# Loads into alternating partitions, pads ahead of the last stage, and a new order, in a linear attention with a mixture of experts

## Chip, cores and metric
One core of a Trainium2 chip. The metric is the device time of one launch in microseconds, the median of several runs.

## What is computed
```python
q_s = softmax(q, axis=-1)                 # q, k, v: 8 batches x 8 heads x 576 rows x 64, fp32
k_s = softmax(k, axis=2)                  # over the 576 rows
attn = einsum('bhsd,bhde->bhse', q_s, einsum('bhsd,bhse->bhde', k_s, v))
x = attn.transpose(0, 2, 1, 3).reshape(4608, 512)
idx = argmax(x @ w_gate, axis=1)          # 8 experts; gate = the largest softmax probability
y[t] = relu(x[t] @ w1[idx[t]]) @ w2[idx[t]]      # w1: 8 x 512 x 1024, w2: 8 x 1024 x 512
out = gate[:, None] * y
```

## The kernel before
The program has two stages. The first computes the attention of the eight batches, routes every row to its expert and scatters it, 512 values with its gate and row number (520 columns), into a DRAM buffer `xs` that has a region per expert. The second, `experts`, walks over tiles of up to 384 rows of `xs`, multiplies them with their expert's weights (each fp32 product as three products of a high and a low part) and scatters the result to `out`. In between, SP fills the 128 rows behind each expert's last row with zeros, the pads (L1232 to L1235), and waits for them before it loads the first tile (`xload`, L1181).

A batch has 576 = 4.5 x 128 rows. Before the change `rows` (L138) cuts them in two contiguous blocks: one half of the partitions (0 to 63, or 64 to 127) holds five rows each, the other half four. k and v have the fives in the lower half; q has them in the lower half in even batches and in the upper half in odd ones, so that the leftover rows of two batches fill one tile of 128. Each tensor of a batch takes two DMAs, one for each half (`lk`, `lv`, `lq`); the first batch's k takes four. All are issued by SP, whose queue also carries parts of the first expert's w1 (L654) and w2 (L665). k has four buffers, v has two (VS) and q has one (QT), so a q load waits for the exponentials of the batch before.

Per batch: VectorE takes the maximum of k over the rows in pieces (`f0`: L292, L293; `f1`: L296, the fifth row of the lower half), PE transposes it, VectorE reduces it (L305), PE spreads it over the partitions (L310), VectorE subtracts it (L326) and ScalarE takes the exponential (L330): five instructions each, four for a pair of heads (KS, KE: 512 columns) and one for the fifth rows (KR, ER: 64 partitions, 512 columns). ScalarE copies v to VT beside columns of ones (`vp` L162, `vq` L165). PE multiplies k and v (L355), five slots x 8 heads; the ones give the sums. For q VectorE takes the maximum of a row (L425, one instruction per batch), GpSimd subtracts it (L430) and ScalarE takes the exponentials, of one slot already on the untransposed rows (L444). A tile of 128 rows is transposed on PE (TR, L470), copied by ScalarE (EX, L475), multiplied with kv and the gate weights (MM, L482), divided on VectorE (DE, RE, EV: L490 to L501) and routed by some fifteen small VectorE steps (R0 to RH); POOL scatters it (PU, L610). After the last batch VectorE computes the tables that the second stage walks by (T1 to T8). T1 also writes `padi`, the row at which each expert's pad begins (L754). The first 384 rows of expert 0 already go through their first layer here (L1 to L3: L711 to L718).

The order of all this is a list written out by hand, `ORDER` (L29): each word names a step, and `Plan.emit` issues the steps in that order, so the list sets the order on every engine and in SP's queue. At the border to the second stage all engines meet. PE then multiplies two dummy tiles (`first(0)`, `first(1)`, L995), transposes the first tile (`tr`, L935), and runs a third dummy before the loop over the experts (L949, L965).

Of the kernel before, what the change touches and what calls it, by code (L numbers as in the profile page):

```python
# [16 lines left out]
P = 128  # L17
# [16 lines left out]
LV KM0 VP MM LV KS MM N0 DE N1 VQ RE KM1 N2 LV EV KM2 TR KM3 DE QM TR EX G0 EX KM4 G1 ER G2 RE QS KS EV KV G3 KE KR KE MM KS QS
QE LS QE KV DE KM0 QE KV QE RE KS VQ LQ MM R0 VP LQ KS CZ KM0 KV LV LK TR EV LK LV TR EX KM1 R8 N0 KM2 DE R1 RE R9 N1 MM KE RC
R3 EV EX N2 KM3 MM DE R4 RE QM TR TR EX R5 G0 EX EV KM4 G1 QS ER QMR MM KE KS DE KV RB QE QS KS QE RE TR R6 EV QSR KE KV KR QE
RH G2 DE QE R7 RE_ RE KS VP LQ KV EV LQ LK KS KV LK RG LS LV KE TR WG RA G3 RD ER R0 MM KM0 VQ EX R8 N0 DE RF R1 PU N1 TR EX KM0
MM N2 PU R3 RE R4 KM1 QM VQ KV RH PU KE G0 KE R5 KV R9 EX EV KE QS KM2 WH RC MM DE RB RE G1 R6 EV G2 RA QE RE_ DE QS KM3 QE TR
RE RD RG PU EV QE MM QE KM0 EX KV LQ G3 LQ DE VP RF RE PU TR KM0 WG KV EV PU MM EX N0 KM1 TR LS PU MM DE N1 EX R0 RE R8 N2 EV TR
R1 R7 MM DE R3 RE R4 EV RH WL EX TR QM WH G0 EX WL WG R9 LK G1 KM2 LK WH KM4 LV QMR QS LV DE KM3 KS KM4 WH KS G2 PU KE RE KR KE  # L40
MM KS G3 QS ER KS QE KV QSR KR QE EV KE KV WL KE KS R5 KV DE KS KE WL QE KS KV QE RB RE PU KM0 TR ER LQ MM VQ LQ EV WG EX LV VP
N0 KS MM LV RC RD WG DE RE_ N1 TR WG RA RG RE RF DE EV PU TR EX N2 KM0 TR MM PU LS RE EX KV R0 PU KM1 EX R8 QM G0 KE PU KM2 KE
KV KE G1 KV R1 EV QS VQ WH TR R3 DE KM3 MM R9 RC RE R6 R4 QE RE_ R7 KM4 RA EV QS QE R5 KV KS EX WL WH MM RB DE KR RG RD RH ER RE
G2 RF KS PU QE EV TR QE G3 KS PU LQ KE MM WG DE KS WH LQ EX RE PU N0 TR EV TR EX N1 MM DE WL N2 RE EV TR LS WL MM DE R0 RE EX EV
WH PU G0 R8 R6 EX DE MM R1 RE R7 R9 R3 VP R4 EV RH PU R5 TR RB RC MM RE_ DE RD RA RG RF RE PU QM G1 KV KE KE G2 PU EX KV G3 EV
# [38 lines left out]
def attention_moe(ctx: ExitStack, tc: tile.TileContext, q, k, v, w_gate, w1, w2, xs, out):  # L84
# [51 lines left out]
    HALF = (slice(0, REM), slice(REM, P))  # L136

    def rows(src, b, i, fives):  # L138
        n = SLOT if i == fives else FULL
        lo = REM * (SLOT if fives == 0 else FULL) if i else 0  # L140
        return n, src[b, :, lo:lo + REM * n, :].rearrange("h (p j) d -> p h j d", j=n)

    def load(b):
# [20 lines left out]
        def vq():  # L164
            ACT(VT[i][:REM, :, FULL // 2 * VW:FULL // 2 * VW + D], o.vs[:REM, :, FULL, :], AF.Copy)  # L165
# [11 lines left out]
        add("VQ", b, 0, ACTE, vq, [("LV", b, 0)] + rng("KV", b - 2, NP))  # L177
# [7 lines left out]
    TS(ident, ji, 0.0, None, op0=ALU.is_equal)  # L185
    ones = cst.tile([E, E], F32, name="ones")
# [40 lines left out]
    def consts():  # L227
        for g in range(B // 2):
            for i in range(2):
                base = (2 * g + i) * S  # L230
                lo = i * (FULL + 1)
                for h in range(2):
                    n = SLOT if h == i else FULL
                    start = base + (REM * (SLOT if i == 0 else FULL) if h else 0)
                    iota(tok[HALF[h], g, lo:lo + FULL], pattern=[[1, FULL]], base=start, channel_multiplier=n)
                    if h == i:
                        iota(tok[HALF[h], g, FULL:FULL + 1], pattern=[[1, 1]], base=start + FULL, channel_multiplier=n)
# [23 lines left out]
    def more_consts():  # L261
        TS(before, ji, 0.0, None, op0=ALU.is_gt)
# [20 lines left out]
    def kmax(b):  # L283
# [11 lines left out]
        def f1():  # L295
            TT(o.km[:REM], o.km[:REM], o.kt[:REM, :, FULL, :], op=ALU.max)  # L296
# [17 lines left out]
        add("KM1", b, 0, DVE, f1, [("LK", b, 0 if b else 2), ("KM0", b, parts - 1)])  # L314
        add("KM2", b, 0, PE, f2, [("KM1", b, 0)], take="tr", until=[("KM3", b, 0)])
        add("KM3", b, 0, DVE, f3, [("KM2", b, 0), ("KM4", b - 2, 0)])
        add("KM4", b, 0, PE, f4, [("KM3", b, 0)], take="tr", until=rng("KS", b, NP - KS_POOL[b]) + [("KR", b, 0)] + ([("KB", b, 0)] if KS_POOL[b] else []))

    def kval(b):
# [3 lines left out]
        def sub(h0, h1, r, j0, j1):  # L323
            t = o.kt[:r, h0:h1, j0:j1, :]
            mb = o.mb.rearrange("p c (i d) -> p (c i) d", i=2)
            TT(t, t, mb[:r, h0:h1, None, :].to_broadcast([r, h1 - h0, j1 - j0, D]), op=ALU.subtract)  # L326

        def ex(h0, h1, r, j0, j1):
            t = o.kt[:r, h0:h1, j0:j1, :]
            ACT(t, t, AF.Exp)  # L330
# [15 lines left out]
        def kv(c):  # L346
# [108 lines left out]
    def xtiles(b):  # L455
# [279 lines left out]
    def tables():  # L735
# [75 lines left out]

        add("T0", z, 0, PE, t0, [("R7", *done[z, SLOT])], take="sm", until=[("T1", z, 0)])
# [61 lines left out]
    with tc.tile_pool(name="qs", bufs=1, space=PSUM) as qs, tc.tile_pool(name="bx", bufs=1) as bx:  # L874
# [8 lines left out]
                            XT=XT, PT=PT, PH=PH, PY=PY, ident=ident, ones16=ones16, tab=tab, zr=zr, padi=padi, w1=w1, w2=w2, xs=xs, out=out, **vars(I0))  # L883
# [5 lines left out]
def experts(nc, tc, g):  # L889
# [10 lines left out]
    sB, sBT, sPad = sem("sb"), sem("sbt"), sem("spad")  # L900
# [273 lines left out]
    def sp():  # L1174
# [57 lines left out]
        for n in range(E):  # L1232
            row = e.value_load(g.padi[0:1, n:n + 1], min_val=0, max_val=E * RS)  # L1233
# [45 lines left out]
```

## Time and profile before
| | us |
|---|---|
| median of 3 runs (lowest, highest) | 669.83 (668.38, 672.86) |
| the profiled execution | 669.31 |
| its span, first to last instruction | 667.4 |
| first stage, to the landing of the last scatter | 226.94 |
| border, to PE's first transpose | 245.26 |
| PE busy in the span | 588.9 |
| mean granted TensorE clock, share of 2.4 GHz | 0.944 |

Times in the profile run from the first instruction. A busy PE is not PE at its peak. A wait for several events is put down to the one that came last.

### The profile page before, as it was taken

To read this page: it belongs to the slowest core of one execution; us is meant where nothing else is said; L and a number is where in the kernel's file an instruction comes from. 1 tells how busy PE (TensorE), PEld (TensorE's weight loads), DVE (VectorE), ACT (ScalarE), POOL (GpSimd) and SP (SyncE) were. 2 spreads that over 40 slices of the span, in tenths; PEclk is the share of its full clock that TensorE was granted. 3 is DMA by queue.
4 is the path that set the end of the run, shared out by engine and by line. 5 is a ranking of instruction groups with operands and counts; after the bars stand their busy time and mean duration, and the time that the engine had idled before them with its cause. 6 is when DMAs were issued, how large, how long until landed. Compare 5 with 4: busy or idle time off the path is not lost.

```text
span 667.4 us, 11339 instructions
## 1 busy us (share of the span) xinstructions
PE 588.9 (88%) x3766; PEld 523.4 (78%) x3767; DVE 330.6 (50%) x704; ACT 257.0 (39%) x519; POOL 134.6 (20%) x218
## 2 busy tenths in 40 slices
PE   3777676878779679999999999999999999999993
PEld 1556565767678469898989898989989898898993
DVE  4665684876858404326442323233751662653472
ACT  0555564565544012224422222214432542442552
POOL 4120133656634301101010101010101101101010
PEclk9687786889999789999999999999999999999998
DMA  9999999997453279210661203020462165044000
GB/s 184 205 198 205 215 220 246 214 232 184 160 184 141 101 200 318 52 45 17 204 185 35 62 17 78 16 63 16 100 235 63 44 184 176 11 154 157 16 19 4
DMA packets 64716, 86.09 MB, mean 129 GB/s; under 512 B 8623, under 2 KB 50095, under 8 KB 64048
## 3 DMA queue, kind: packets, MB, share of 16 engines
q1 hardware_dynamic: 58688, 66.71, 42.8%
q0 software_dynamic: 6000, 19.03, 7.5%
q8 instruction: 15, 0.25, 0.2%
q14 instruction: 13, 0.11, 0.1%
HBM read 63.78 MB, written 22.74 MB: 130 GB/s over the span
## 4 chain that ended last, share of the span: by engine, by line
PE 62%; SPq 1%; DMA 1%; issue 1%; POOL 0%; ACT 0%; POOLq 0%
PE py L965 29%; PE pt L949 16%; PE ph L949 16%; PE py L995 1%; SPq L1233 1%; DMA xt<-xs 0%; SPq L1234 0%; PE pt L935 0%; DMA xs<-xr,posi 0%; DMA xs<-zr 0%; SPq L922 0%; POOL out L1150 0%; SPq L1186 0%; ACT yt L1023 0%; SPq L1256 0%
## 5 line engine op out<-in xcount | busy, mean ns | idle before, releaser
L965 PE MATMUL py<-w2h,hid 128*128 128x512 f32 x576 | 179.7, 389 | 0.0
L965 PEld LDWEIGHTS py<-w2h,hid 128*128 128x128 f32 x576 | 108.1, 188 | 22.1
L1150 POOL DMA_INDIRECT out<-yt,ix x39 | 43.3, 1110 | 352.5 <-ACT yt L1023 352.5
L965 PE MATMUL py<-w2l,hid 128*128 128x512 f32 x288 | 112.1, 389 | 0.0
L1097 DVE SCALAR_TENSOR_TENSOR hid<-pt,hid 128x384 fp32r<-128x384 f32 x56 | 30.9, 558 | 148.9 <-ACT hid L1032 141.0
L1023 ACT ACTIVATE yt<-py,ga 128x512 f32<-128x512 f32 x39 | 26.8, 688 | 150.4 <-PE py L965 133.8
L482 PE MATMUL xp<-kx,qTs 128*128 128x146 f32 x256 | 45.3, 328 | 23.7 <-DVE xr L501 16.5
L965 PEld LDWEIGHTS py<-w2l,hid 128*128 128x128 f32 x288 | 54.1, 188 | 10.7
L1097 DVE SCALAR_TENSOR_TENSOR hid<-ph,hid 128x384 fp32r<-128x384 f32 x56 | 31.2, 558 | 59.1 <-ACT hid L1032 59.1
L482 PEld LDWEIGHTS xp<-kx,qTs 128*128 128x128 f32 x256 | 39.4, 218 | 26.6 <-DVE xr L501 13.2
L1032 ACT ACTIVATE hid<-ph 128x384 fp32r<-128x384 f32 x56 | 27.6, 492 | 65.7 <-PE ph L949 65.7
L1032 ACT ACTIVATE hid<-pt 128x384 fp32r<-128x384 f32 x56 | 27.6, 492 | 65.0 <-PE pt L949 62.6
L610 POOL DMA_INDIRECT xs<-xr,posi x36 | 39.5, 1098 | 50.5 <-DVE posi L599 18.5
L1087 DVE STREAM_TRANSPOSE xx<-xb 128x1536 f32<-128x1536 f32 x14 | 40.7, 2908 | 7.7 <-DVE gs L1093 5.7
L949 PE MATMUL pt<-xl,w1h 128*128 128x384 f32 (+1 forms) x224 | 43.8, 317 | 0.0
L949 PE MATMUL ph<-xh,w1l 128*128 128x384 f32 (+1 forms) x224 | 43.6, 316 | 0.0
L949 PE MATMUL pt<-xh,w1l 128*128 128x384 f32 (+1 forms) x224 | 43.6, 316 | 0.0
L949 PE MATMUL ph<-xh,w1h 128*128 128x384 f32 (+1 forms) x224 | 43.6, 316 | 0.0
L949 PE MATMUL ph<-xl,w1h 128*128 128x384 f32 (+1 forms) x224 | 43.6, 316 | 0.0
L949 PE MATMUL pt<-xh,w1h 128*128 128x384 f32 (+1 forms) x224 | 43.6, 316 | 0.0
L430 POOL TENSOR_TENSOR qs<-qt,qm 128x1024 f32<-128x1024 f32 (+1 forms) x16 | 23.5, 1484 | 77.3 <-DVE qm L425 26.4
L355 PE MATMUL kv<-vt,kt 128*64 128x65 f32 (+1 forms) x640 | 35.3, 257 | 3.4 <-ACT vt L162 3.1
(205 smaller groups left out, 954.5 us busy)
## 6 DMA issues: line engine op xcount, KB each, us to landing
raw<-in_moe_w SPq DMA_DIRECT2D x10, 2048.0 KB, 8.2
xb<-xs SPq DMA_DIRECT2D x32, 192.0 KB
qt<-in_q SPq DMA_DIRECT2D x8, 640.0 KB
vs<-in_v SPq DMA_DIRECT2D x8, 640.0 KB, 14.3
kt<-in_k SPq DMA_DIRECT2D x7, 640.0 KB, 15.1
qt<-in_q SPq DMA_DIRECT2D x8, 512.0 KB
vs<-in_v SPq DMA_DIRECT2D x8, 512.0 KB, 15.9
kt<-in_k SPq DMA_DIRECT2D x7, 512.0 KB, 17.1
```

Source lines behind the costliest of these rows:

```text
L355: nc.tensor.matmul(o.kv[i * D:(i + 1) * D, c, lo:lo + D + 1], o.kt[:r, 2 * c + i, j, :], VT[b % 2][:r, 2 * c + i, at:at + D + 1], start=Fa ...
L430: nc.gpsimd.tensor_tensor(o.qs[:, j0:j1].rearrange("p j h d -> p h j d"), o.qt[:, :, j0:j1, :], o.qm[:, :, j0:j1, None].to_broadcast([P, H ...
L482: nc.tensor.matmul(xv[:, c, :KW], o.qT[i][:, c, :], kx[:, c, :], start=True, stop=True)
L610: s = nc.gpsimd.indirect_dma_start(out=xs, out_offset=bass.IndirectOffsetOnAxis(ap=n.pi[:, t - t0:t - t0 + 1], axis=0), in_=xr[:, t, :], i ...
L949: m = e.matmul(ph, wt[:, c, f * P:(f + 1) * P], xt[:, c, :w], start=(n == 0), stop=(n == 3 * NC - 1))
L965: m = e.matmul(g.PY[u], ht[:, f, u * P:(u + 1) * P], wt[:, f, :], start=(n == 0), stop=(n == 3 * NF - 1))
L995: m = e.matmul(g.PY[u], ht[:, f, u * P:(u + 1) * P], wt[:, f, :], start=(n == 0), stop=(n == 3 * NF - 1))
L1023: m = e.activation(g.YT[u], g.PY[u], AF.Copy, scale=g.GA[:, u:u + 1]).wait_op(sPY[u], cu[u], GE)
L1032: e.activation(g.HH[:, f, :], g.PH[f][:, :W], AF.Relu).wait_op(sPH[f], it, GE).then_inc(sHH[f], 1)
L1087: e.transpose(g.XX, g.XB.rearrange("p t (a c) -> p c t a", c=NC)).wait_op(sB, b80, GE)
L1097: e.scalar_tensor_tensor(g.HL[:, f, :], g.PH[f][:, :W], 0.0, g.HH[:, f, :].bitcast(F32), op0=ALU.max, op1=ALU.subtract).wait_op(sHH[f], it ...
L1150: e.indirect_dma_start(out=g.out, out_offset=bass.IndirectOffsetOnAxis(ap=g.IX[:, u:u + 1], axis=0), in_=g.YT[u], in_offset=None, bounds_c ...
```

## The change
Nine consecutive rows now belong to a pair of partitions. The even partition takes the first five, the odd one the last four; for k both take five, so the fifth is there twice. Each tensor still takes two DMAs, one for the even and one for the odd partitions, each of 64 partitions with a step of two. Doubling k's fifth row does no harm to the maximum; in the product it must count once, so v's first slot is zero on the odd partitions (VS is cleared once) and so is the column of ones beside it, which is set from a new constant `par`, the parity of the partition. With every partition holding five rows of k, the steps KR and ER go, and KS and KE take 640 columns. In odd batches q's fives go to the odd partitions; the transposed copy of the leftover tile then sorts even and odd columns into two halves. The row numbers `tok` follow the new layout.

The pads move from `experts` to a step PD of the first stage, after T1, without a wait of their own. `ORDER` is replaced as a whole; its last lines now hold PD.

```diff
-    def rows(src, b, i, fives):
-        n = SLOT if i == fives else FULL
-        lo = REM * (SLOT if fives == 0 else FULL) if i else 0
-        return n, src[b, :, lo:lo + REM * n, :].rearrange("h (p j) d -> p h j d", j=n)
+    ODDS = (slice(0, P, 2), slice(1, P, 2))
+
+    def rows(src, b, lo, hi, hs=slice(0, H)):
+        return src[b, hs].rearrange("h (m r) d -> m h r d", r=FULL + SLOT)[:, :, lo:hi, :]
...
-            n, src = rows(k, b, p % 2, 0)
-            nc.sync.dma_start(o.kt[HALF[p % 2], hs, :n, :], src[:, hs])
+            lo = p % 2 * FULL
+            nc.sync.dma_start(o.kt[ODDS[p % 2], hs], rows(k, b, lo, lo + SLOT, hs))
...
-            n, src = rows(v, b, p, 0)
-            nc.sync.dma_start(o.vs[HALF[p], :, :n, :], src)
+            nc.sync.dma_start(o.vs[ODDS[p], :, p:, :], rows(v, b, p * SLOT, p * FULL + SLOT))
...
-            n, src = rows(q, b, p, i)
-            nc.sync.dma_start(QT[HALF[p], :, :n, :], src)
+            n = FULL if p else SLOT
+            nc.sync.dma_start(QT[ODDS[p ^ i], :, :n, :], rows(q, b, p * SLOT, p * SLOT + n))
...
+    par = cst.tile([P, 4], F32, name="par")
+    RED(par[:, 0:1], ident[:, 1:P:2], op=ALU.add, axis=AX.X)
+    TS(par[:, 1:2], par[:, 0:1], -1.0, 1.0, op0=ALU.mult, op1=ALU.add)
...
+        nc.vector.memset(VS[i][:, :, 0, :], 0.0)
+        nc.vector.tensor_copy(VT[i][:, :, 0], par[:, 1:2].to_broadcast([P, H]))
...
-            TT(o.km[:REM], o.km[:REM], o.kt[:REM, :, FULL, :], op=ALU.max)
+            TT(o.km, o.km, o.kt[:, :, FULL, :], op=ALU.max)
...
-        add("KR", b, 0, DVE, lambda: sub(0, H, REM, FULL, SLOT), [("KM4", b, 0)])
-        add("ER", b, 0, ACTE, lambda: ex(0, H, REM, FULL, SLOT), [("KR", b, 0)])
...
-                add("KS", b, c, DVE, lambda c=c: sub(2 * c, 2 * c + 2, P, 0, FULL), [("KM4", b, 0)])
+                add("KS", b, c, DVE, lambda c=c: sub(c), [("KM4", b, 0)])
...
-            ACT(o.qT[i], o.qP[i], AF.Copy if FULL - ON_ACT[b] <= slots[i] < FULL else AF.Exp)
+            to = o.qT[i] if slots[i] < FULL else o.qT[i].rearrange("p c (a m) -> p c m a", a=2)
+            at = o.qP[i] if slots[i] < FULL else o.qP[i].rearrange("p c (m a) -> p c m a", a=2)
+            ACT(to, at, AF.Copy if FULL - ON_ACT[b] <= slots[i] < FULL else AF.Exp)
...
+        def pads():
+            for e in range(E):
+                row = nc.sync.value_load(padi[0:1, e:e + 1], min_val=0, max_val=E * RS)
+                d = nc.sync.dma_start(xs[bass.ds(row, P), :], zr)
+                for other in written:
+                    tc.declare_no_dep(d.ins, other.ins, reason="distinct rows")
+                written.append(d)
+
+        add("PD", z, 0, SP, pads, [("T1", z, 0)])
...
-        for n in range(E):
-            row = e.value_load(g.padi[0:1, n:n + 1], min_val=0, max_val=E * RS)
-            e.dma_start(g.xs[bass.ds(row, P), :], g.zr).then_inc(sPad, 16)
-        e.wait_ge(sPad, 16 * E)
         xload(0)
...
-PU RE_ RF RD L3 R7 VL PU T0 L1 L2 RG R9 VH RH RC T1 RH PU L3 RA T2 RF RE_ T3 PU L1 L2 L3 T5 PU L1 L2 PU IM PU L3 L2 T6 T7 L1 L3
+T1 RF R5 T2 PD RB L3 T3 L1 PU RA RE_ RD T5 PU L1 L2 PU VH VH L3 T6 RG VL L2 L1 RF L3 PU T7 VL L1 L2 PU L3 T8 IN VL L2 L3
```

SP at the start of the program, before: the loads of the first batches' q (qt), v (vs0, vs1 of even and odd batches) and k (kt), with partitions, heads and columns of each.
```order
L169 DMA qt_90<-in_q 64x8x320
L169 DMA qt_90<-in_q 64x8x256
L158 DMA vs0_88<-in_v 64x8x320
L158 DMA vs0_88<-in_v 64x8x256
L153 DMA kt_189<-in_k 64x8x320
L153 DMA kt_189<-in_k 64x8x256
L153 DMA kt_198<-in_k 64x8x320
L153 DMA kt_198<-in_k 64x8x256
L158 DMA vs1_89<-in_v 64x8x320
L254 DMA wg_105<-in_moe_w_gate 64x4x8 x2
```
The same place after the change, from the first q on.
```order
L166 DMA qt_95<-in_q 64x8x320
L166 DMA qt_95<-in_q 64x8x256
L151 DMA kt_188<-in_k 64x8x320 x2
L155 DMA vs0_93<-in_v 64x8x320
L155 DMA vs0_93<-in_v 64x8x256
L151 DMA kt_197<-in_k 64x8x320 x2
```
The second k comes before the first v, and both halves of k have 320 columns.

SP at the end of the first stage, before: the last loads of that stage, the meeting of the engines (NO_OP, branch) and the first pad, which reads padi.
```order
L692 DMA xt<-xs 128x520 x3
L665 DMA raw_2077<-in_moe_w 128x2x512 x4
L884 NO_OP
L1256 UNCONDITIONAL_BRANCH
L1233 TENSOR_LOAD padi
L1233 ISA x2
L1234 ISA
L1234 DMA xs<-zr 128x520
```
After the change, from the same loads on to the first pad.
```order
L694 DMA xt<-xs 128x520 x3
L667 DMA raw_2090<-in_moe_w 128x2x512 x4
L816 TENSOR_LOAD padi
L816 ISA x2
L817 ISA
L817 DMA xs<-zr 128x520
```
The eight pads (one is shown) stand ahead of the meeting; behind the meeting SP's next rows are now the table reads and `xload`.

VectorE around the step that writes padi, before.
```order
L602 RECIPROCAL xr_116<-own 128x3
L590 TENSOR_REDUCE own<-pe 128x2
L752 TENSOR_SCALAR c_169<-cn,r_128 128x1
L753 COPY c_169<-cn 128x7
L754 TENSOR_TENSOR padi<-cn,padc 1x8
L718 SCALAR_TENSOR_TENSOR hid<-ph_2263,hid 128x384
L583 TENSOR_SCALAR cm<-own 128x2
L757 TENSOR_SCALAR g<-c_169,thr 128x8
```
The same place after the change.
```order
L592 TENSOR_REDUCE own<-pe 128x2
L578 TENSOR_TENSOR acc_5_2291<-acc_3_2282,own 128x8
L754 TENSOR_SCALAR c_170<-cn,r_137 128x1
L755 COPY c_170<-cn 128x7
L756 TENSOR_TENSOR padi<-cn,padc 1x8
L601 TENSOR_TENSOR posi<-own,cm 128x3
L759 TENSOR_SCALAR g<-c_170,thr 128x8
L589 TENSOR_TENSOR rs<-rk,oh 128x16
```
padi now follows the last count of rows (acc) at once; routing steps that stood ahead of it stand behind it.

## Rows read from the trace of the kernel before
**Rows 1.** The page's slices: the span in 40 equal parts of 16.7 us; busy tenths of PE, VectorE and the DMA engines, and GB/s.
```profile
PE   3777676878779679999999999999999999999993
...
DVE  4665684876858404326442323233751662653472
...
DMA  9999999997453279210661203020462165044000
GB/s 184 205 198 205 215 220 246 214 232 184 160 184 141 101 200 318 52 45 17 204 185 35 62 17 78 16 63 16 100 235 63 44 184 176 11 154 157 16 19 4
```
**Rows 2.** Windows over the first stage: length, busy us (and instructions) of PE, PE's weight loads, DVE, ACT, POOL, then the granted TensorE clock, the DMA share and GB/s.
```profile
0.00:120.00 120.00, 80.55 (x730) 63.38 (x733) 71.48 (x179) 59.16 (x143) 30.73 (x82) 0.82 1.10 211
120.00:227.00 107.00, 83.58 (x748) 73.30 (x742) 78.19 (x293) 55.26 (x136) 57.18 (x84) 0.92 0.63 174
0.00:227.00 227.00, 164.13 (x1472) 136.68 (x1473) 149.67 (x472) 114.42 (x279) 87.91 (x165) 0.87 0.88 194
```
**Rows 3.** The chain that ended last: start, us, what.
```profile
224.22 2.72 DMA xs<-xr,posi
...
228.26 0.47 SPq L1233
...
238.98 0.39 SPq L922
...
242.12 3.10 DMA xt<-xs
245.26 2.83 PE pt L935 x12
...
651.70 5.50 PE py L965 x24
```
**Rows 4.** Windows by the rate of the DMA engines, columns as in rows 2: the first load's first half microsecond, the loads behind it, two stretches of loads alone, loads beside scatters, a load of w2 (128 partitions), a load of raw weights (128 partitions).
```profile
2.90:3.40 0.50, 0.30 (x1) 0.00 (x0) 0.00 (x0) 0.00 (x0) 0.41 (x5) 1.00 1.00 365
3.40:5.00 1.60, 0.00 (x0) 0.00 (x0) 0.00 (x0) 0.00 (x0) 1.23 (x11) 1.00 1.13 232
30.00:40.00 10.00, 7.72 (x43) 5.15 (x42) 6.50 (x11) 5.17 (x15) 0.00 (x0) 0.85 1.15 197
50.00:60.00 10.00, 6.61 (x85) 5.64 (x82) 5.30 (x15) 4.50 (x10) 0.00 (x0) 0.84 1.13 204
...
148.00:150.00 2.00, 2.00 (x12) 1.67 (x14) 2.00 (x4) 1.10 (x2) 0.42 (x1) 0.50 1.03 379
194.00:195.00 1.00, 0.50 (x4) 0.50 (x5) 0.00 (x0) 0.45 (x1) 0.82 (x4) 1.00 1.12 387
251.00:255.00 4.00, 4.00 (x22) 3.57 (x20) 3.23 (x3) 0.69 (x1) 0.99 (x1) 1.00 1.01 426
```
**Rows 5.** VectorE's maximum of q, one per batch: all eight by their line (shortest, median and longest ns, first and last start), then the second, sixth, seventh and eighth as the timeline has them.
```profile
L425 DVE TENSOR_REDUCE qm<-qt x8: 2233/2280/2286, 14.9 to 171.4; 128x32 f32<-128x2048 f32 x8
...
42.40 2.29 DVE L425 TENSOR_REDUCE qm<-qt 128x32 f32<-128x2048 f32 x1 [4.42 <-DMA qt<-in_q]
...
125.80 2.27 DVE L425 TENSOR_REDUCE qm<-qt 128x32 f32<-128x2048 f32 x1
...
147.17 2.27 DVE L425 TENSOR_REDUCE qm<-qt 128x32 f32<-128x2048 f32 x1
...
171.37 2.23 DVE L425 TENSOR_REDUCE qm<-qt 128x32 f32<-128x2048 f32 x1
```
**Rows 6.** Waits over the span, and those of SP's own queue: us in total, times, longest.
```profile
ACT vt L165 <- DMA vs<-in_v: 23.5, 4, 15.6
...
DVE kp L292 <- DMA kt<-in_k: 15.7, 6, 4.7
DVE qm L425 <- DMA qt<-in_q: 14.4, 4, 4.4
...
SPq L169 <- ACT qs L444: 38.3, 7, 10.6
```
**Rows 7.** DMA issues (count, KB each, us to landing) and groups of instructions of the first stage (busy us, mean ns of one, idle us before them).
```profile
kt<-in_k SPq DMA_DIRECT2D x7, 640.0 KB, 15.1
...
kt<-in_k SPq DMA_DIRECT2D x7, 512.0 KB, 17.1
...
L326 DVE TENSOR_TENSOR kt<-kt,mb 128x512 f32<-128x512 f32 (+1 forms) x40 | 25.8, 671 | 1.5 <-PE mb L310 1.5
...
L671 DVE TENSOR_TENSOR w2l<-raw,w2h 128x1024 fp32r<-128x1024 f32 x4 | 4.7, 1206 | 0.0
...
L330 ACT ACTIVATE kt<-kt 128x512 f32<-128x512 f32 (+1 forms) x40 | 23.6, 620 | 3.8 <-DVE kt L326 3.7
L475 ACT ACTIVATE qTs<-qT 128x512 f32<-128x512 f32 x36 | 21.1, 591 | 29.6 <-PE qT L470 22.4 <-PE xp L482 6.9
L444 ACT ACTIVATE qs<-qt,qm 128x64 f32<-128x64 f32 x64 | 16.7, 334 | 3.4 <-DVE qm L425 3.4
L162 ACT ACTIVATE vt<-vs 128x1024 f32<-128x1024 f32 x16 | 16.0, 1050 | 11.4 <-DMA vs<-in_v 10.5 <-POOL qs L430 1.0
```
**Rows 8.** The timeline around the border: VectorE writes padi, PE ends its dummy products and waits.
```profile
210.31 0.14 DVE L754 TENSOR_TENSOR padi<-cn,padc 1x8 int32<-1x8 f32 x1
...
240.60 0.39 PE L995 MATMUL py<-w2h,hid 128*128 128x512 f32 x1
245.26 2.83 PE L935 MATMUL pt<-ident,xt 128*128 128x128 f32 x12 [4.27 <-DMA xt<-xs]
```

More of the change, by code (lines that the diff above doesn't have):

```diff
@@ L34 @@
[L34 to L45, printed above, removed]
@@ new lines @@
+LQ LQ RE_ DE RF LV R6 KV RE DE RG LV EV LK KE KV KM0 LK PU WH KV KE RE LS PU KE TR N0 R0 KM0 TR EX PU TR EX R8 N1 MM R1 WH EV N2
+PU R3 KM1 MM R4 DE R7 QM TR EX VQ KM2 EX R5 RA G0 RE QS RB KM3 G1 EV KM4 R9 KE G2 RC RD DE KS QE QS MM KS QE RH G3 WL KE RE KS
+TR KV QE EV WL QE KV KS EX LQ KE LQ KM0 TR LV VP TR LV RE_ DE RF MM RG KM0 PU KV DE KE RE RE EV PU VQ KV KM1 KE LV PU LS MM WG
+EX EV WG LK TR PU R0 EX N0 DE LK R8 R6 MM RE N1 EV N2 TR R1 R7 DE MM R3 RE R4 EV RH PU EX KV QM EX R9 R5 KM2 VP MM KM3 QS TR RB
@@ new lines @@
+QMR G0 EX KV DE R6 RE G1 RD EV QE QS KM4 DE KV RC QE RE KS QSR QE G2 EV QE RA KE KV LS LQ LQ VQ RE_ RF TR R0 WG N0 R8 G3 RG R1
+MM LV PU N1 R9 R3 RC N2 KS MM R7 PU R4 DE KS R5 KS KE KV PU EX RB RE TR RE_ RD EV G0 RH EX PU RG KV RA WH DE RF RE KM0 G1 MM PU
+KE EV TR KM0 PU G2 EX KE TR DE RE PU KM1 G3 MM EV TR WL EX QM MM WH WH WL WG KM2 EX KV VQ DE DE QS RE RE VP EV TR KV KM3 LS MM
+QS EV QE QE R6 PU R0 MM DE R8 R7 EX RE N0 R1 EV QE TR PU R9 QE R3 N1 MM DE EX RC R4 LQ RE RE_ RA N2 EV WL LQ R5 TR WG KM4 RB DE
@@ L231, in consts @@
                 lo = i * (FULL + 1)
[L232 to L237, printed above, removed]
+                iota(tok[:, g, lo:lo + FULL], pattern=[[2, FULL]], base=2 * base, channel_multiplier=FULL + SLOT)
+                iota(tok[HALF[i], g, FULL:FULL + 1], pattern=[[1, 1]], base=base + FULL, channel_multiplier=FULL + SLOT)
         nc.gpsimd.memset(zr, 0.0)
@@ L261, in more_consts @@
     def more_consts():
+        for i in range(2):
+            sl = slice(i * (FULL + 1), i * (FULL + 1) + FULL)
+            TS(tok[:, :, sl], tok[:, :, sl], 0.5, par[:, 2 + i:3 + i], op0=ALU.mult, op1=ALU.add)
         TS(before, ji, 0.0, None, op0=ALU.is_gt)
@@ L313, in kmax @@
             add("KM0", b, i, DVE, lambda i=i: f0(i), [("LK", b, 1 if b else 2 * i + 1), ("KM0", b, i - 1)], take=None if i else "km", until=[("KM2", b, 0)])
-        add("KM1", b, 0, DVE, f1, [("LK", b, 0 if b else 2), ("KM0", b, parts - 1)])
+        add("KM1", b, 0, DVE, f1, [("KM0", b, parts - 1)])
         add("KM2", b, 0, PE, f2, [("KM1", b, 0)], take="tr", until=[("KM3", b, 0)])
         add("KM3", b, 0, DVE, f3, [("KM2", b, 0), ("KM4", b - 2, 0)])
-        add("KM4", b, 0, PE, f4, [("KM3", b, 0)], take="tr", until=rng("KS", b, NP - KS_POOL[b]) + [("KR", b, 0)] + ([("KB", b, 0)] if KS_POOL[b] else []))
+        add("KM4", b, 0, PE, f4, [("KM3", b, 0)], take="tr", until=rng("KS", b, NP - KS_POOL[b]) + ([("KB", b, 0)] if KS_POOL[b] else []))
     def kval(b):
@@ L321, in kval, with sub, ex @@
         kx = KX[b % 2]
[L323 to L329, printed above, removed]
+        def sub(c):
+            t = o.kt[:, 2 * c:2 * c + 2]
+            m = o.mb[:, c].rearrange("p (i d) -> p i d", i=2)
+            TT(t, t, m[:, :, None, :].to_broadcast([P, 2, SLOT, D]), op=ALU.subtract)
+        def ex(c):
+            t = o.kt[:, 2 * c:2 * c + 2]
             ACT(t, t, AF.Exp)
@@ L354, in kv @@
                 for i in range(2):
-                    nc.tensor.matmul(o.kv[i * D:(i + 1) * D, c, lo:lo + D + 1], o.kt[:r, 2 * c + i, j, :],
-                                     VT[b % 2][:r, 2 * c + i, at:at + D + 1], start=False, stop=(c == NP - 1 and j == FULL))
+                    nc.tensor.matmul(o.kv[i * D:(i + 1) * D, c, lo:lo + D + 1], o.kt[:, 2 * c + i, j, :],
+                                     VT[b % 2][:, 2 * c + i, at:at + D + 1], start=False, stop=(c == NP - 1 and j == FULL))
         ks = mine(b, 0, NP)
@@ L882, in attention_moe @@
         g = SimpleNamespace(E=E, RS=RS, N=N, DM=DM, NC=NC, NF=NF, MAXS=MAXS, W1H=W1H[0], W1L=W1L[0], W2H=W2H[0], W2L=W2L[0],
-                            XT=XT, PT=PT, PH=PH, PY=PY, ident=ident, ones16=ones16, tab=tab, zr=zr, padi=padi, w1=w1, w2=w2, xs=xs, out=out, **vars(I0))
+                            XT=XT, PT=PT, PH=PH, PY=PY, ident=ident, ones16=ones16, tab=tab, w1=w1, w2=w2, xs=xs, out=out, **vars(I0))
         with tc.tile_critical():
```

38 lines of the change are left out of this document (21 added, 17 removed).

## Prediction
> **What bounds the kernel now.** I read the page's slices first [rows 1]. In the first nine slices the DMA row stands at 9 throughout and moves 184 to 246 GB/s, while PE and DVE stand at 3 to 8. From the sixteenth slice (250 us) on PE stands at 9, to the last but one. So there are two stages with two limits, and the totals of the page say nothing about either. The windows give the first stage in numbers [rows 2]: in 0 to 120 us the DMA share is 1.10 (packets overlap, so it can pass 1) at 211 GB/s and DVE is busy 71.5 us, 60%. In 120 to 227 us the DMA share is 0.63 and DVE is busy 78.2 of 107 us, 73%. The chain that ended last [rows 3] says what closes that stage: the last scatter lands at 226.94, SP then issues the eight pads until 238.98, loads the first tiles, and from 245.26 PE runs almost without a gap until 657. That last part, some 412 us, is TensorE work that the change leaves alone.
>
> Why are 204 GB/s the limit of the loads? The windows by rate answer [rows 4]. In steady state, with q, k and v alone in the queue, it is 197 to 204 GB/s. The first half microsecond of the first load, with nothing queued before it, runs at 365. With scatters running beside the loads it is 379, a load of w2 into 128 partitions reaches 387 and one of raw weights 426. So neither the DMA engines nor the memory behind them stop at 204. The slow rows are those in which nothing but transfers into 64 neighbouring partitions is under way. The bill for it is the spacing of the batches, seen best in VectorE's q maximum, one per batch [rows 5]: eight of them from 14.9 to 171.4 us, 22.4 us apart. DVE waits for k and q 15.7 and 14.4 us and ScalarE for v 23.5 us, up to 15.6 at once [rows 6]; what waits behind those two in their fixed order doesn't show as a DMA wait.
>
> [...]
>
> **Loads.** One tensor of one batch is 640 + 512 KB [rows 7], 1.18 MB; 24 of them are 28.3 MB, which at 204 GB/s take 138.7 us. The fifth row of k is now loaded twice: 8 x 128 KB, 1.05 MB, so 29.4 MB. The new rate is in no row. Ends: 197 GB/s (149 us, 10 more than now) and 387 (76 us, 63 less). A transfer still holds only 64 partitions and packets of 1 to 1.25 KB, but spreads over the whole range; the nearest row is the unhindered half microsecond at 365, which is short, so I take 300: 98 us. With 1.2 MB of scatters and 0.26 MB of w1 per batch at 387, DMA needs 12.2 + 3.8 = 16 us a batch, under the 22.4 of now. The loads then no longer set the spacing.
>
> **What is late next.** VectorE has 149.7 us of work before 227 us, PE 164.1 [rows 2]. [...] The stretch that shows what they reach when DMA doesn't hold them is 120 to 227 us: DVE 73%, PE 78%. DVE at 73% throughout needs 149.7/0.731 = 204.8 us, 22.2 less than 227. PE as a check: its clock was granted at 0.82 in the first stretch and 0.92 in the second, a mixture of 1.2 and 2.4 GHz; 80.6 x 0.82/0.92 + 83.6 = 155.4 us, over 0.78 gives 199 us, 28 less; without any gain in clock 164.1/0.78 = 210, 17 less. I take the middle one of the three, **-22.2**. Its ends are +5 (1.05 MB more at the old rate) and -40 (DVE at 80%, 187 us).
>
> **Edits on the engines.** The subtraction of the k maximum goes from 40 instructions of 512 columns, 671 ns each, to 32 of 640 [rows 7]. Between 512 columns and the 1206 ns of 1024 that is 1.04 ns a column, so 805 ns: 25.8 us, as now. The exponentials: 620 ns for 512 and 1050 for 1024 give 728, x 32 = 23.3 us against 23.6. The third maximum and the fifth matmul of a head take 128 partitions where they took 64, with the same columns: 0. The copy of the transposed leftover slot writes with a stride: 4 of 36 instructions of 591 ns; at worst each costs as much as eight of 64 columns at 334 ns, +8 us on ScalarE, which is busy 114 of 227 us; I take 0. Seven small DVE instructions and two memsets of 512 columns are new at the start, at most 7 x 0.3 + 2 x 0.7 = 3.5 us; DVE is idle there while the first k arrives (0.00 busy from 2.9 to 5.0 us [rows 4]), so 0, or 3.5 if that cover goes. Fewer iotas on POOL: 0.
>
> **Pads.** They leave the chain: from 228.26 to 238.98 is 10.7 us of SP [rows 3], and xt would land at 245.22 - 10.7 = 234.5. But PE still has the two dummy products of that stage, which end at 240.60 + 0.39 = 240.99 [rows 8], and only then can transpose. PE's wait of 4.27 us is all that goes: **-4.3**, a little more if the transposes, 2.83 us after that idle time, also run faster. Late next is PE itself. In their new place the pads wait on SP for padi, which VectorE writes at 210.31 [rows 8]. Nothing is queued behind them on SP before the experts. They need the 10.7 us again, and between padi and the last scatter's landing lie 16.5. In the new order about as many VectorE rows (44 against 40) follow padi before the experts, so they are hidden with some 5 us to spare. If padi came that much later in the stage, each further microsecond would count in full. Their 2.1 MB share the DMA engines with the last scatters, at 387 GB/s 5.5 us spread over 9: 0, at worst 1.
>
> **Sum**, from the profiled execution: 669.3 - 22.2 - 4.3 = 642.8. The median of the timed runs is 669.8, so the profiled one stands for them. I say **643**.
>
> **Rivals.**
> *One q tile.* All batches share one q tile, so the next q can't be loaded before the exponentials of the last are done. For it: SP waits 38.3 us for them in all, up to 10.6 at once [rows 6], and the last two spacings of q maxima are 21.4 and 24.2 us although DMA was no longer full, while the four before them average 20.9 [rows 5]. If the spacing stays 20.9, the gain is 7 x (22.4 - 20.9) = 10 us: 655. Against it: the exponentials stand where the order, now a new one, puts them.
> [...]
> *More than forecast.* The engines close up to DVE at 80%: 669.3 - 40 - 4.3 = 625. The new order may have room for it, since loads stop being late.
> *Slower.* Alternating rows read 1280 of every 2304 bytes, with gaps, and write every second partition. If that lowers the rate, all 29.4 MB pay: at the 184 GB/s of the page's first slice [rows 1] 159.6 us, +20.9, less 4.3: 686. It decides below 196 GB/s, where loads take 149.7 us, 11 more than now, and the whole is slower by over 1% after the pads' gain.
>
> **Chances.** Forecast 0.50 (its own range 632 to 652), one q tile 0.20, rate unchanged 0.12, more than forecast 0.13, slower 0.05. One per cent of 669.8, 6.7 us, is about what a measurement can tell from no change. Faster by more than that: 0.50 + 0.20 + 0.13 = 0.83; within: 0.12; slower: 0.05. The range takes in the first, the second and the fourth: 622 to 664.
>
> **What would show it.** Right: in the first 100 us windows of loads alone at 260 GB/s or more; q maxima about 19 us apart; DVE busy over 70% of the front; the front closing near 205 us; SP loading xt right after the last scatter and PE going from the dummy products to the transposes without a wait. Wrong: loads at 200 GB/s as before; spacing near 21 us with idle DMA (then it is the q tile); pads landing after the last scatter; or TensorE losing clock in the experts' part, which the sum leaves at 412 us.

## The result, and the profile after

The changed kernel takes **628.19 us** (median of 4 runs, 627.09 to 630.4) against 669.25 us before (4 runs; three of them gave the 669.83 of the table): a ratio of 0.938, 95% interval 0.934 to 0.942. The forecast was 643, within 622 to 664. The profiled execution took 630.40 us with a span of 628.6. An execution more than 1.5% above the fastest of its kernel is left out of the ratios of this document, but not out of its medians and ranges.

The page's slices (15.7 us each now; PE, VectorE, DMA) answer to [rows 1].
```profile
PE   3788688789787999999999999999999999999993
...
DVE  5999676797572332255323231427626652752572
...
DMA  8989956752556813034702020111550552044000
```
The DMA row stands at 8 or 9 for five slices, where it stood at 9 for nine, VectorE stands at 9 in the second to the fourth, and PE at 9 from the fourteenth on, where it was the sixteenth. The windows answer to [rows 2] and, by rate, to [rows 4]; columns as there.
```profile
0.00:100.00 100.00, 70.42 (x766) 56.78 (x768) 77.81 (x205) 63.59 (x150) 36.16 (x82) 0.93 0.90 294
...
10.00:20.00 10.00, 9.19 (x35) 4.53 (x35) 7.32 (x9) 3.55 (x11) 2.93 (x2) 1.00 1.08 362
40.00:50.00 10.00, 8.60 (x127) 7.83 (x128) 9.50 (x20) 8.90 (x25) 2.93 (x2) 1.00 1.08 364
```
Where loads are queued they now run at 362 to 364 GB/s, where [rows 4] had 197 to 204. The 294 of the first 100 us is a mean over stretches at 362 to 367 and others at less (87 GB/s in 80 to 90 us). VectorE's q maxima and the waits (us in total, times, longest) answer to [rows 5, 6].
```profile
L425 DVE TENSOR_REDUCE qm<-qt x8: 2275/2280/2286, 12.3 to 139.9; 128x32 f32<-128x2048 f32 x8
...
DVE xr L503 <- DMA xs<-xr,posi: 16.4, 4, 4.9
...
DVE kp L295 <- DMA kt<-in_k: 3.2, 2, 1.8
...
DVE qm L425 <- DMA qt<-in_q: 0.5, 2, 0.4
...
SPq L166 <- ACT qs L444: 37.7, 7, 12.1
```
The maxima stand (139.9 - 12.3) / 7 = 18.2 us apart instead of 22.4. VectorE's waits for k and q fell from 15.7 and 14.4 us to 3.2 and 0.5. Its largest wait for a transfer is now one of 16.4 us, in four pieces, for scatters that still read a buffer of x. SP's wait for the one q tile (the last line) is about as long as before.

The chain at the border answers to [rows 3, 8] (start, us, what). Before, two short products open the border, and the experts' first product begins at 253.58:
```profile
228.15 1.03 PE L1000 MATMUL ph<-ones 128*128 128x512 bf16 x2 [6.32 <-SPq L884]
...
253.58 6.26 PE pt L949 x36
```
After:
```profile
177.47 0.72 SPq L816
...
190.59 2.32 DMA xs<-zr
...
193.90 1.04 PE ph L1011 x2
194.94 13.12 PE py L1006 x48
208.06 1.44 PE pt L946 x12
...
214.98 1.04 PE pt L960 x6
```
The front closes at 193.90 instead of 228.15, **34.25 us earlier**. From there to the first expert it is 214.98 - 193.90 = 21.08 us instead of 25.43, **4.35 less**. Both together, 38.6, are nearly all of the span's 38.8; the experts' part changed by 0.2. And the last link in front of the border is a pad: the pads left one place on the path and came to stand at another.

### The profile page after: what moved, and what is told of

The parts are those of the page before. It is cut to its first block, busy times and chain, and to the rows that moved or that the text cites. A ratio compares the mean times of both kernels' runs of the same rounds, so it can differ in the third digit from the quotient of the medians.

```text
span 628.6 us, 11335 instructions
## 1 busy us (share of the span) xinstructions
PE 572.3 (91%) x3766; PEld 512.8 (82%) x3767; DVE 329.5 (52%) x706; ACT 255.6 (41%) x511; POOL 130.7 (21%) x210
## 4 chain that ended last, share of the span: by engine, by line
PE 74%; DVE 10%; DMA 7%; issue 4%; ACT 2%; SPq 2%; POOL 1%; POOLq 0%; DVEq 0%; ACTq 0%
PE py L976 31%; PE pt L960 16%; PE ph L960 16%; DMA xs<-xr,posi 5%; PE py L1006 3%; DVE kt L329 2%; DVE xr L503 2%; PE xp L484 2%; DVE kp L295 1%; DMA qt<-in_q 1%; PE ph L713 1%; PE kv L357 1%; DMA kt<-in_k 1%; PE qT L470 1%; DVE km L296 1%
## 5 line engine op out<-in xcount | busy, mean ns | idle before, releaser
L1034 ACT ACTIVATE yt<-py,ga 128x512 f32<-128x512 f32 x39 | 26.8, 687 | 149.3 <-PE py L976 133.7
L976 PEld LDWEIGHTS py<-w2l,hid 128*128 128x128 f32 x288 | 54.1, 188 | 10.7
L484 PE MATMUL xp<-kx,qTs 128*128 128x146 f32 x256 | 42.7, 314 | 12.1 <-DVE own L560 5.5
L484 PEld LDWEIGHTS xp<-kx,qTs 128*128 128x128 f32 x256 | 37.3, 208 | 14.3 <-issue 10.9
L612 POOL DMA_INDIRECT xs<-xr,posi x36 | 35.7, 992 | 40.9 <-issue 10.3
L960 PEld LDWEIGHTS pt<-xh,w1h 128*128 128x128 f32 x224 | 37.0, 189 | 1.2
L960 PEld LDWEIGHTS ph<-xh,w1h 128*128 128x128 f32 x224 | 36.5, 189 | 0.0
```

The costliest lines, as they stand in the source:

```text
L484: nc.tensor.matmul(xv[:, c, :KW], o.qT[i][:, c, :], kx[:, c, :], start=True, stop=True)
L612: s = nc.gpsimd.indirect_dma_start(out=xs, out_offset=bass.IndirectOffsetOnAxis(ap=n.pi[:, t - t0:t - t0 + 1], axis=0), in_=xr[:, t, :], i ...
L960: m = e.matmul(ph, wt[:, c, f * P:(f + 1) * P], xt[:, c, :w], start=(n == 0), stop=(n == 3 * NC - 1))
L976: m = e.matmul(g.PY[u], ht[:, f, u * P:(u + 1) * P], wt[:, f, :], start=(n == 0), stop=(n == 3 * NF - 1))
L1034: m = e.activation(g.YT[u], g.PY[u], AF.Copy, scale=g.GA[:, u:u + 1]).wait_op(sPY[u], cu[u], GE)
```

## Experiments

**Neighbouring partitions again.** Only the places change; loads, order and all instructions stay (with `par` and the row numbers to match, and without the sorting of the leftover tile).
```diff
-    ODDS = (slice(0, P, 2), slice(1, P, 2))
+    ODDS = HALF
```


> The changed kernel with one thing undone: the two loads of a pair go to the lower and the upper 64 partitions instead of the even and the odd ones. Bytes, number, order and shapes of the loads, every engine's instructions and the pads stay as changed. If the spread over the partitions sets the rate: loads near 200 GB/s in the first 100 us (as before the change; 294 with the change, pauses included), packets of 1,280 bytes near 111 ns instead of 59, q maxima 25 us apart, time 660 to 672 us. If the rate came from the nine-row pieces or from the order of the list: near 360 GB/s in the steady stretches and 628 us.

665.77 us, ratio to the kernel before 0.996 (0.992 to 0.9995). A window and the q maxima of this run:
```profile
0.00:100.00 100.00, 65.87 (x578) 51.09 (x580) 60.02 (x146) 47.01 (x110) 20.89 (x59) 0.81 1.10 203
...
L425 DVE TENSOR_REDUCE qm<-qt x8: 2275/2286/2287, 15.4 to 179.8; 128x32 f32<-128x2048 f32 x8
```
203 GB/s at a DMA share of 1.10, maxima 23.5 us apart: the old rate and with it nearly the old time, though pads, list and nine-row pairs are all there. The spread over the partitions carries 665.8 - 628.2 = 37.6 of the 41 us (the two were not run side by side; the ratios to the kernel before, 0.996 and 0.938, say the same). The bytes, the pieces of 1 and 1.25 KB and the addresses read are equal in the two, so it isn't the reading side.

**The pads alone**, moved in the kernel before (the step PD behind T2, the loop in `experts` gone).
```diff
-... RH PU L3 RA T2 RF RE_ T3 ...
+... RH PU L3 RA T2 PD RF RE_ T3 ...
```


> The kernel before with the pads alone moved ahead of the table, loads and the rest of the list as before. By the step on the pads: 4.3 us less, 665 us, since the front runs on for over 15 us behind the row numbers of the pads. Rival: the pads' 10 us of issues hold up SP's queue or the last scatters, the front ends as much later, and the time stays at 669 us.

665.52 us, ratio 0.997 (0.993 to 1.001), where the kernel before has 667.62 beside it: 2.1 us less by the medians, between 5 less and 1 more. The chain at the border shows the step itself:
```profile
221.15 2.73 DMA xs<-xr,posi
225.11 1.03 PE ph L1009 x2
...
238.68 1.44 PE pt L944 x12
...
245.60 4.53 PE pt L958 x26
```
From the front's end to the first expert 245.60 - 225.11 = 20.5 us, against 25.4: the wait is gone. Here a scatter ends the front, not a pad. The wait was worth 4.3; whether the pads cost something in front of it, or nothing, the interval leaves open.

**The pads back** in `experts`, in the changed kernel; the list loses PD.
```diff
-T1 RF R5 T2 PD RB L3 T3 ...
+T1 RF R5 T2 RB L3 T3 ...
```


> The changed kernel with the pads back in the last section. Since with the change the pads land about 1 us behind the last scatter, the front should end 1 us earlier without them and the transposes wait 4.3 us more: 631 to 632.5 us. Rival: the pads hold the end of the front by several us, and what they save there they cost in front of it: 628 us, no difference.

630.82 us (629.73 to 633.06), 2.6 more by the medians. The two were not run side by side, and the intervals of their ratios overlap (0.938 to 0.951 here, 0.934 to 0.942 for the changed kernel), so the 2.6 is not clear of noise. The time came out 0.2 below the expected range, and by other parts than expected. The front's end and the border:
```profile
188.77 0.60 PE L1002 MATMUL ph<-ones 128*128 128x512 bf16 x2 [1.98 <-SPq L886]
...
203.15 3.20 DMA xt<-xs
206.39 2.84 PE pt L937 x12
...
215.56 1.56 PE pt L951 x9
```
In this run padi is written at 175.30 and the front ends at 188.77, 13.5 us behind it; in the changed kernel it is 177.30 and 193.90, 16.6 (15.8 in its second profile). So the front ends 2.4 to 3.1 us later behind padi with the pads in it, where 1 was expected. From the end of the front to the experts it is 215.56 - 188.77 = 26.8 us, 5.7 more. The difference, 2.6 (3.2 by the second profile), fits the medians; the two profiled executions themselves are only 0.6 us apart, because padi came 2.0 us earlier in this one.

Part of those us is seen on VectorE, which computes the second stage's table behind padi. Its write of padi and the last step of that table's fields, first in the changed kernel, then here:
```profile
177.30 0.14 DVE L756 TENSOR_TENSOR padi<-cn,padc 1x8 int32<-1x8 f32 x1
...
184.84 0.17 DVE L796 SCALAR_TENSOR_TENSOR fld<-on,last 8x23 f32<-8x23 f32 x1
```
```profile
175.30 0.14 DVE L756 TENSOR_TENSOR padi<-cn,padc 1x8 int32<-1x8 f32 x1
...
180.00 0.17 DVE L796 SCALAR_TENSOR_TENSOR fld<-on,last 8x23 f32<-8x23 f32 x1
```
The same steps take 7.5 us with the pads beside them and 4.7 without: between some of them VectorE now stands idle, up to 1.7 us at once. What holds it there isn't shown. With the list of before, the same stretch is no longer with the pads (5.8 us in the run below) than without (6.3 in the kernel before).

**The list of before**, with the new loads (KR and ER left out of it, PD behind T2).

> The changed kernel with the list of before (entries that no longer exist left out, the pads behind their row numbers). Loads, layout and instructions as changed. If the rate alone carries the front: 628 to 633 us. If the rate is worth something only with a list in which the engines take the data as it now comes: half of the 34 us in the front, about 645 us. If the list alone carried it: 665 us.

633.83 us (632.65 to 634.95), just above the first of the three expected ranges. By the medians the new list is worth 5.6 us beside the new rate (not run side by side; all four times lie above all of the changed kernel's); the old one, written for loads at 204 GB/s, already gets the rest.
```profile
0.00:100.00 100.00, 74.58 (x753) 60.80 (x754) 76.41 (x198) 61.10 (x148) 31.80 (x76) 0.88 0.82 269
...
ACT L163 <- DMA vs<-in_v: 15.4, 1, 15.4
```
With the old list VectorE is 76% busy in the first 100 us, almost the 78% of the new one. What the old list still gives away is in part seen in ScalarE's one wait of 15.4 us for v, which the changed kernel doesn't have. In part it stands on VectorE: the same 474 instructions of the front take 155.1 us of its time instead of 148.6, since a few small steps that take 0.2 us elsewhere take up to 3.0. What held those isn't shown.

**The changed kernel again**, as a base for the next three on one chip.

> The changed kernel unchanged, run once more beside the next three so that differences of a few us can be read against it: 628 us.

627.76 us (625.64 to 629.68), ratio 0.937.

**Three k tiles**, the control for the next.
```diff
-KTB = 4
+KTB = 3
```


> The changed kernel with three k tiles instead of four, as a control for the next run, which needs their space; a k load then waits for the sums over k three batches back, and stands in the list at the first place where these are issued. If the loads' lead of four batches is not needed: 628 us. If it is: some of the waits for k come back, 632 to 640 us.

629.05 us (628.62 to 629.58), ratio 0.939: by the medians the fourth k tile gave 1.3 us, which is within the noise.

**A third buffer of x**, in the space of that k tile.
```diff
-    XR = [xa_pool.tile([P, FULL + i, RW], F32, name=f"xr{i}", bufs=1) for i in range(2)]
+    XR = [xa_pool.tile([P, SLOT, RW], F32, name=f"xr{i}", bufs=1) for i in range(2)] + [ka_pool.tile([P, SLOT, RW], F32, name="xr2", bufs=1)]
...
-        xr = XR[odd]
+        xr = XR[b % 3]
...
-("PU", b - 2, t)
+("PU", b - 3, t)
```


> As the control with three k tiles, and with a third buffer for the rows x that VectorE writes and the indirect scatters read. In the changed kernel VectorE waits 16.4 us in four places for scatters that still read the buffer. If the scatters' landing now bounds the front: 5 to 12 us less than the control. If those waits stand beside PE's or ACT's work: no difference from the control.

619.7 us (616.33 to 628.76), ratio to the kernel before 0.923 (0.920 to 0.927), where the changed kernel beside it has 0.937 (0.934 to 0.940): 9.4 us less than the control. So the buffers of x, which the scatters still read, are what bound next. This is the version with the lowest median. Its times spread widely, and its profiled execution was the longest of the six, 628.76 us: there too VectorE waits for no scatter and is 82% busy in the first 100 us, yet the front ends only at 193.46, at a granted clock of 0.92. The third buffer removes the wait; that alone did not shorten every execution, and why this one stayed long isn't known.

**Pads on two queues**, in the changed kernel.
```diff
-            for e in range(E):
+            for e in range(E // 2):
...
+                row = nc.scalar.value_load(padi[0:1, e:e + 1], min_val=0, max_val=E * RS)
+                d = nc.scalar.dma_start(xs[bass.ds(row, P), :], zr)
...
+        add("PA", z, 0, ACTE, apads, [("T1", z, 0)])
```


> The changed kernel with four of the eight pads issued on ACT's queue, at the same place, the other four on SP's. If the pads' issues on SP's queue, 13 us in a row, hold the end of the front: it ends 13.5 us behind the pads' row numbers (as with the old pads) instead of 16.6, 625 to 626.5 us. Rival: the last scatters end it anyway, and ACT's own work is held up by the issues: 628 us or a little more.

627.50 us (624.22 to 628.72), ratio 0.936: no difference from 627.76. padi is written at 176.82 and the front ends at 192.86, still 16.0 us behind it. The chain says why:
```profile
184.97 5.81 PE ph L713 x24
...
190.80 0.50 ACT hid L717
...
192.86 0.60 PE ph L1021 x2
```
Now first-layer products and their evictions end the front. The front ends 0.6 us sooner behind padi than in the changed kernel. The expectation of 13.5 us had taken the run without pads for one in which only the issues on SP are gone. But this other chain starts from VectorE's table, and from padi (176.82) to the table's step L796 (184.24) it takes 7.4 us here as well, against 4.7 without pads. The control with three k tiles and its pads on one queue shows the same: there, too, these products end the front, 16.0 us behind padi. So it isn't SP's issuing alone that the pads cost.

**Both halves at once.** The neighbouring halves again, but in the first batch the upper half's loads of k and q are issued on ScalarE's queue beside the lower half's on SP's.
```diff
-            nc.sync.dma_start(o.kt[ODDS[p % 2], hs], rows(k, b, lo, lo + SLOT, hs))
+            (nc.sync, nc.scalar)[p % 2 if b < 1 else 0].dma_start(o.kt[ODDS[p % 2], hs], rows(k, b, lo, lo + SLOT, hs))
```


> The kernel of the halves experiment, in which in the first batch alone the loads of k and q to the upper 64 partitions are issued on ACT's queue, beside those to the lower 64 on SP's, so that both halves are loaded at the same time. If the rate hangs on how many different partitions' rows are in flight together, and not on the alternation as such: near 360 GB/s in the first 15 us and the first q maximum near 12.3 us, as with the change. If a transfer to 64 neighbouring partitions is slow by itself, whatever runs beside it (or one queue's order is kept): near 204 GB/s there and the first q maximum near 15.4 us.

665.99 us in its one execution; the first q maximum starts at 15.19 us. Windows in which both queues have loads to do:
```profile
4.00:8.00 4.00, 0.00 (x0) 0.00 (x0) 1.12 (x2) 1.28 (x1) 2.74 (x24) 1.00 1.10 222
11.00:13.00 2.00, 1.18 (x5) 0.99 (x6) 0.76 (x3) 0.00 (x0) 0.00 (x0) 1.00 1.08 340
```
The halves run with one queue has 220 and 207 in the same windows, the changed kernel 303 and 362. So with two queues 340 is reached in one stretch, but not in the other. The packets of each queue (q1 is SP's, lower half; q10 is ScalarE's, upper half; packets, MB, share of the engines) tell the two stretches apart. At 4 to 5 and at 5 to 6.5 us:
```profile
q10 hardware_dynamic: 191, 0.24, 106.9%
q1 hardware_dynamic: 10, 0.01, 2.1%
...
q1 hardware_dynamic: 217, 0.28, 95.9%
q10 hardware_dynamic: 41, 0.03, 12.8%
```
At 11 to 13 us:
```profile
q1 hardware_dynamic: 327, 0.40, 63.5%
q10 hardware_dynamic: 285, 0.28, 44.8%
```
At 222 GB/s the queues take turns, and most packets of a moment go to one half; at 340 the packets of both halves are in flight together. That speaks for the first expectation: the rate hangs on how many different partitions are being written together, and a load to neighbours isn't slow by itself. But the q maximum started only 0.2 us sooner than with one queue (15.4), since the halves were seldom mixed so evenly (207 and 220 GB/s at 2 to 6 and 6 to 10 us, 300 at 10 to 14), and why the queues take turns stays open.

**A second q tile**, with three k tiles. This kernel leaves the fifth rows of the even batches out of the result; instructions and bytes are the same but for one memset on GpSimd.
```diff
-            [...] rng("QS", b - 1, 2) + rng("QE", b - 1, 2 * NP) [...]
+            [...] rng("QS", b - 2, 2) + rng("QE", b - 2, 2 * NP) [...]
```


> The control with three k tiles, and with a second q tile, so that a q load waits for the batch two back (the fifth rows of the even batches are left out of the result; the instructions and the bytes are the same, plus one memset on POOL). SP waits 37.7 us in seven places for ACT's reads of the one q tile in the changed kernel. If these waits bound the front, as the rival of one q tile said: 5 to 10 us less than the control's 629. If the q rows come in time anyway (VectorE waits 0.5 us for them): 628 to 630 us.

622.82 us (620.6 to 626.98), ratio 0.932 (0.925 to 0.939); the control had 0.939 (0.936 to 0.942). 6 us less by the medians, with intervals that overlap a little. The window of the first 100 us and the wait for scatters, of the control and then of this run:
```profile
0.00:100.00 100.00, 68.08 (x771) 56.09 (x773) 77.99 (x208) 64.28 (x154) 36.46 (x82) 0.94 0.89 293
...
DVE xr L506 <- DMA xs<-xr,posi: 17.9, 4, 5.1
```
```profile
0.00:100.00 100.00, 73.71 (x873) 60.38 (x874) 85.22 (x227) 70.16 (x168) 41.66 (x87) 0.98 0.99 329
...
DVE xr L508 <- DMA xs<-xr,posi: 7.7, 3, 4.1
```
VectorE goes from 78% to 85%, although it waited only 0.5 us for q by name. It isn't free of the x waits in this run either: they fell from 17.9 us in the control to 7.7, so the two causes aren't cleanly apart.

**Three x buffers and pads on two queues**, the two edits together (and three k tiles).

> The kernel with three buffers for x and three k tiles, with the pads on two queues. By the runs before: 619.7 us, and at most 1 us less, since layer 1 of the table's side work stands right behind the pads at the front's end. If the pads hold more now that the front is shorter: 616 to 617 us.

622.14 us (615.62 to 631.27), ratio 0.930 (0.924 to 0.935): not better than three x buffers alone, and no gain from the second queue is shown. Its profile, the first 100 us and the border:
```profile
0.00:100.00 100.00, 77.48 (x911) 63.54 (x913) 88.14 (x242) 72.88 (x177) 42.24 (x89) 0.98 0.94 313
...
181.82 0.61 PE ph L1024 x2
```
This is the profile of the shortest of its six executions, 615.62 us. No wait of VectorE for scatters is left in it, VectorE is 88% busy in the first 100 us, and the front ends at 181.82.

## Why the prediction was right, and which terms were off

**The bound, and the rate: right, and shown.** 204 GB/s were the loads' limit, and it came from 64 neighbouring partitions: with everything else kept, putting the halves back gives 203 GB/s and 665.8 us. The rate was taken as 300 and is 362 to 364, near the 365 of the first half microsecond before [rows 4]. What the runs show is that it hangs on the partitions: 203 GB/s into neighbouring ones, 362 to 364 into alternating ones, with the same bytes and pieces. What neighbours share that holds them at 203 isn't shown. The size didn't matter for the sum, since at either rate the loads stop setting the spacing. The forecast of 643 itself was too high: 628.19 lies below its own range of 632 to 652 and nearest to the 625 of *more than forecast*, which had a chance of 0.13. The stated range held because it took that rival in.

**The front: the mis-sized term.** The step put VectorE at 73% throughout, -22.2 us; it was -34.25. The window of the whole front after:
```profile
0.00:194.00 194.00, 147.99 (x1473) 126.53 (x1475) 148.62 (x474) 113.20 (x271) 84.08 (x157) 0.93 0.72 243
```
VectorE's work was 148.6 us, within 1.1 of what was taken, and 148.6 / 193.9 is 77%. What failed is the sentence that 120 to 227 us shows what the engines reach "when DMA doesn't hold them". DMA did hold VectorE there, only not by a load. Rows of before that the prediction hadn't read, VectorE's waits for scatters in 120 to 227 us, then in the whole span:
```profile
DVE xr L501 <- DMA xs<-xr,posi: 9.2, 5, 3.6
...
DVE xr L501 <- DMA xs<-xr,posi: 11.9, 6, 3.6
```
9.2 of the 28.8 idle us were waits for scatters. Without those, 78.2 / (107 - 9.2) is 80%. In the runs VectorE gets there: with three x buffers and split pads the front of the shortest execution ends at 181.82 with VectorE at 82%, with the second q tile at 186.73 with 80%. So 73% was no ceiling of the order. But the scatters are not what gave the missed 12 us: in the changed kernel VectorE waits 16.4 us for them, 4.5 more than before, and stands at 77% all the same. Its idle time in the front fell from 227 - 149.7 = 77.3 to 194 - 148.6 = 45.4 us, by 32: its waits for k and q fell by 26.4, those for scatters rose by 4.5, and the rest, idle time beside other engines' work, fell by 10. How that 10 divides between the new list, TensorE's clock and loads that come earlier isn't settled; by the run with the old list, at 633.8, the new one is worth some 5.6.

PE's busy time in the front fell from 164.1 to 148.0 us with the same products (1472 and 1473 by the windows), and the granted clock, a mixture of stretches at 0.50 and at 1.00 of full speed, rose from 0.87 to 0.93. The check by PE had taken 155.4, and with it 199 us; that end of the three was the nearer one.

**The pads: the gain behind the border right, the cover wrong.** PE's wait of 4.27 us went and 4.35 were gained there, but for other reasons in part. The transposes, which had begun behind idle time, took 1.44 us instead of 2.83. The products ahead of them took longer, as the window of 194 to 199 us shows:
```profile
194.00:199.00 5.00, 5.00 (x12) 3.68 (x13) 1.35 (x2) 0.00 (x0) 0.00 (x0) 0.50 0.48 131
```
These first 5 us stand at a granted clock of 0.50, behind 3.91 us in which PE had nothing to do, and three of these products take 1.28 us; in the run with the pads back three take 0.7, as here at 0.98 in 199 to 208 us, and the transposes, behind 6.1 idle us, stand at 0.50. "Hidden with some 5 us to spare" failed. The pads took 177.47 to 192.91, 15.4 us and not 10.7, and the front ended 16.6 us behind padi where before it was 17.8. They landed last, which the prediction had named as a sign of being wrong, and by the run without them the front ends 2.4 to 3.1 us later for them, in part because VectorE's table takes longer beside them. So the move as a whole was worth less than the 4.3 of the sum: 2.6 by the medians in the changed kernel and 2.1 in the kernel before, neither clear of noise.

**Edits on the engines: right.** The subtraction and the exponential over 640 columns:
```profile
L329 DVE TENSOR_TENSOR kt<-kt,mb 128x640 f32<-128x640 f32 x32 | 24.9, 812 | 1.7 <-PE mb L313 1.6
L333 ACT ACTIVATE kt<-kt 128x640 f32<-128x640 f32 x32 | 22.9, 732 | 15.4 <-DVE kt L329 14.6 <-issue 0.8
L477 ACT ACTIVATE qTs<-qT 128x512 f32<-128x512 f32 x36 | 22.8, 646 | 25.1 <-PE xp L484 11.8 <-PE qT L470 9.0 <-PE kvT L382 2.5
```
812 and 732 ns where 805 and 728 were worked out from [rows 7]. The third maximum takes 682 ns on 128 partitions (L299, median) where it took 677 on 64 (L296 before). The strided copy of the transposed leftover, put between 0 and 8 us, cost ScalarE 22.8 - 21.1 = 1.7 (the longest copy takes 1.1 us), and these copies have 25 us of idle time before them.

**The rivals.** *Slower*, and the chance of 0.12 for a rate unchanged, fell with the 362 GB/s. *One q tile* was wrong as a forecast of 655, since the spacing fell to 18.2; but as a mechanism it is real. A second tile gives about 6 us by the medians, once the loads are fast, though in a kernel that leaves rows out and with x waits that fell too. *More than forecast* came nearest; VectorE reached 77% of its 80%, and 80 to 82% where the waits for scatters were shorter or gone.

## What to carry to other kernels

When a load into half the partitions runs at about half the rate of its neighbours into all (here 197 to 204 GB/s beside 387), change which partitions it takes before anything else (here that gave 362 to 364); the bytes and the pieces can stay. Before a busy share is taken as what an engine can reach, subtract every wait for a transfer in that stretch, stores and scatters too (here 9.2 of 28.8 idle us). A step that is moved off one chain has to be followed to the end of the chain it joins, with its issues at the pace they have beside what runs there (here 15.4 us for the eight pads instead of 10.7).

## What the hardware showed

- Loads to 64 alternating partitions run at 362 to 364 GB/s, to 64 neighbouring ones at 203, with equal bytes and pieces; in the first 100 us the median piece of 1,280 bytes takes 55 ns against 111 in the kernel before.
- Two halves on two queues ran at 222 GB/s where the queues took turns and at 340 where the pieces of both were in flight at once; with one queue it is 220 and 207 there.
- The same kernel differs by several us between executions; in the two that were profiled all of it lies in the front: the profile of the second run of the changed kernel has 625.78 us in place of 630.40, and its front ends at 189.21 instead of 193.90. Its front as one window, against 148.0 us of PE and 0.93 above:
```profile
0.00:189.21 189.21, 141.92 (x1473) 121.80 (x1474) 148.36 (x474) 113.16 (x271) 84.61 (x157) 0.95 0.74 249
```
PE spends 141.9 us on the same products instead of 148.0. The shorter front goes with the higher granted clock; which of the two is the cause isn't shown.
